# Sums over partitions by a block of ones: moving a layer norm's reductions from GpSimd to TensorE in an FNet and feed-forward kernel

## The chip, the core and the metric

The kernel runs on one core of a Trainium2 chip. The time is that of one execution on the device, in microseconds (us). The kernel before takes 683.24 us (median of three runs, 682.79 to 684.26). A core has five engines that run side by side, each through its own list of instructions in order: TensorE (PE in the profile, with its weight loads as PEld), VectorE (DVE), ScalarE (ACT), GpSimd (POOL) and SyncE (SP), which here only issues DMA transfers. An engine that has to wait for another holds up everything behind it in its own list.

## The reference

The input x has 2048 positions of 512 numbers, float32. Two sublayers follow one another, each with a layer norm ahead and a residual sum behind:

```python
a = einsum("bsd,ed->bse", x, dft_hid_re)          # x is the layer-normed input here
b = einsum("bsd,ed->bse", x, dft_hid_im)
y = einsum("ts,bse->bte", dft_seq_re, a) - einsum("ts,bse->bte", dft_seq_im, b)
...
h  = x + A(_layernorm(x), ...)                     # Fourier mixing, above
h2 = h + B(_layernorm(h), w1, w2)                  # silu(h @ w1) @ w2, F = 1792
```

The layer norm of a position needs the mean and the variance over its 512 numbers. All products are wanted in float32 accuracy.

## The kernel before, in words

**Accuracy.** Every operand of a product is split in two: ScalarE rounds it to TensorE's float32r format (the part `...h`), and VectorE subtracts to get the remainder (`...l`). `three` (lines 200 to 204) then issues three products of 128x128 by 128x512: high by high (L202), high by remainder (L203), remainder by high (L204). `rounded` (lines 149 to 160) makes the two parts; L152 is ScalarE's half and L156 or L158 VectorE's. So ahead of nearly every product stand one ScalarE and one VectorE instruction of 128x1024, and in the profile their tiles are called `ph` and `pl`.

**Stages.** The sequence mixing comes first, as `plain(0, 0)`, `fast(1, 0)`, `fast(0, 1)`, `fast(1, 1)` (the first number is the cosine or sine matrix, the second the half q of the output positions). The blocks are multiplied with seven products in place of eight where possible, which costs VectorE sums and differences (L593, L618 to L630). `mix(0)` and `mix7(1)` apply the hidden matrices to the halves, add the input, and so make h. `norm_h` (line 839) makes the second layer norm of a half. `up` and `down` are the feed-forward products. The order of the calls is: plain, fast(1,0), mix(0), fast(0,1), fast(1,1), mix7(1), up(0), down(0), up(1), down(1). The norm of half 0, called by mix(0), therefore runs on the other engines while TensorE is in fast(0,1) and fast(1,1), and that of half 1 while it is in up(0).

**The second layer norm.** After the mixing h lies transposed: 128 of the 512 numbers on the partitions, four such groups beside one another, and 512 positions along the free axis. The block of 512 positions is called tau, 0 or 1 within a half. A sum over the 512 numbers of a position is hence two additions of VectorE (L834, L835) and a sum over the partitions, which GpSimd does (L836, in `total`). This is done twice for each tau, once for the mean and once for the variance; `center` (L851) and `square` (L857) lie between. Then one row of variances goes through DRAM to be laid out over the partitions (L863, L868), VectorE makes the reciprocal roots (`root`, `finish`), they go through DRAM again (L877, L880) and `scale` multiplies (L885).

**The order.** Nothing is scheduled while it runs. Each piece of work is a function with a planned time: `step` (line 208) puts a group of products at the running clock of TensorE, 0.2265 us each, with pieces ahead of it by a lead and behind it by a delay; `at(t, f)` puts a piece at a time. `program` returns all pieces sorted by planned time, and every engine but SyncE gets its instructions in exactly that order. The planned times only fix this order: an engine starts a piece as soon as its inputs are there. The pieces of `norm_h` are at `start + d`, with `start = clock[0] + NORM_US[q][tau]` and the d of the list at L893. Pieces ahead of a product use `halves(lead, make)`: the rounding 2.2 us (GAP_US) before the lead, the remainder at the lead, most often PREP_US = 8 us.

**Pages.** All big tiles in SBUF are pages of 4 KB per partition, 51 of them (PAGES). `Plan` runs the whole program once without issuing anything, notes in which order pages are taken and when they are planned to be free, and gives each new tile the page that is planned to have been free longest. A load by SyncE waits until the last user of its page is done, and SyncE's later loads wait behind it. The loads for a group of products in `fast` (`load`, L597 to L600, issued by L328) come in threes, and `prep` (L602) makes differences of them in place (L593).

**PSUM.** `banks` (L146) gives one of four tiles of two banks each.

Of the kernel before, what the change touches and what calls it, by code (L numbers as in the profile page):

```python
# [15 lines left out]
P = 128  # L16
# [8 lines left out]
NP = NF // 2  # L25
SKEW = 2
JJ = (2, 3, 0, 1)
KEPT = (0, 1)
EPS = 1e-5
PAGES = 51  # L30
WARM = 12
MM_US = 0.2265
PREP_US = 8.0
LEADS = (((0, 14, 9, 5), (1, 15, 9, 3), 12, 11.5),
         ((0, 25, 14, 7), (1, 18.5, 7.5, 4), 17.5, 16))
LOAD_US = 18.0
FETCH_US = 13.0
NORM_US = (14, 84), (1, 14)
GAP_US = 2.2
FIRST = 0, 1, 2, 4.1, 5.15, 4.7, 5.05, 8.8, 8.2, 20, 8.9, 9.9, 21.9, 25.1, 30.5, 15  # L40
ADD_US = 15.1, 7
SUMS_US = (21.4, 5.9, 6.8, 3.7), (26.4, 5.8, 4.4, 1.2)
KEEP_US = 2, 1
FREE_US = {None: 2.0, "matmul": 4.0, "dma_start": 10.0}
ORDERED = (mybir.EngineType.PE, mybir.EngineType.DVE, mybir.EngineType.Activation, mybir.EngineType.Pool)

# [87 lines left out]
def program(nc, page, keep, small, psum, dram, x, xT, seq, hid, ffn, out):  # L134
# [244 lines left out]
    def plain(c, q):  # L379
# [71 lines left out]
        def add(name, a, b):  # L451
            nc.vector.tensor_tensor(made[name], a, b, op=ALU.add)
# [57 lines left out]
        order = [(2, 2), (1, 2), (3, 2), (1, 3), (2, 3), (3, 3), (6, 2), (7, 2), (6, 3), (7, 3), (4, 2), (4, 3), (5, 2), (5, 3)]  # L510
        for n, jj in order:
            key = "A", c, q, n, jj
            before = halves({6: 8, 4: 4.5, 7: 3.5, 5: 6.5}.get(n, PREP_US), lambda key=key, n=n: round_raw(key, -1.0 if n == 6 else 1.0))
            if n == 2:
                before += tiles_x(jj)
            if n <= 3:
                before.append((LOAD_US + {1: 0, 2: 0, 3: 4}[n], lambda n=n, jj=jj: load_b(n, jj)))
            if n == 1:
                before += [(PREP_US - 1.8, lambda jj=jj: negate(1, jj)), (PREP_US - 1.8 - 0.2, lambda jj=jj: plus(5, jj)),
                           (-1.5, lambda jj=jj: t2(jj))]  # L520
            if n == 3:
                before += [(PREP_US + 3, lambda jj=jj: negate(3, jj)), (PREP_US + 3 - 0.2, lambda jj=jj: plus(7, jj))]
            if n == 6:
                before.append((8 - 2.5, lambda jj=jj: plus(4, jj)))
            after = {
                (1, 3): [(0, lambda: copy_out("p1", acc[1]))],
                (4, 3): [(4, lambda: add("u2", acc.pop((c, q, 1, 0)), made["u2"]))],
                (2, 3): [(0, lambda: copy_out("11", acc.pop((c, q, 0, 0)))), (25, lambda: add("11", made["11"], made.pop("p1")))],
                (6, 3): [(0, lambda: copy_out("u2", acc[1]))],
                (7, 3): [(7, lambda: minus("22", acc[7])), (9, lambda: minus("u2", acc.pop(7)))],  # L530
                (5, 3): [(0, lambda: copy_out("w", acc.pop(1))), (5, lambda: add("22", made["22"], made["w"])),
                         (5.5, lambda: add("w", acc.pop((c, q, 0, 1)), made["w"]))],
            }.get((n, jj), [])
            step(12, lambda n=n, jj=jj: prod(n, jj), before, after)
        at(clock[0] + 6, ready)
        for n, v in enumerate(((0, 0), (1, 0), (1, 1), (0, 1))):
            at(clock[0] + 6 + 1.2 * n, lambda v=v: store_c(q, *v))
        for jj, (t, t3) in enumerate(((86, 96), (92, 112), (37, 54), (49, 63))):
            at(t, lambda jj=jj: early(("s", jj), lambda: sums_x(jj)))
            for n, (d, which) in enumerate(((t + 2.5, (4,)), (t3, (1, 2, 3)))):  # L540
                at(d, lambda jj=jj, n=n, which=which: early(("s", jj, n), lambda: round_s(jj, late["s", jj], which)))
                at(d + 1.5, lambda jj=jj, n=n: rest(late.pop(("s", jj, n))))
# [192 lines left out]
    def mix7(q):  # L735
# [55 lines left out]
            nc.vector.tensor_tensor(h[q, tau, e], bank[name], h[q, tau, e], op=ALU.add)  # L791

        outs = {1: [(0, 0, "Y")], 2: [(0, 0, "X")], 6: [(0, 1, "Y")], 7: [(1, 1, "V")], 5: [(1, 1, "Y")], 4: [(0, 1, "V")], 3: [(1, 0, "Y")]}
        lead = {1: 8.5, 2: 3.5, 6: 6, 7: 9, 5: 14, 4: 4, 3: 4.5}
        t = clock[0] - 43
        for n, (c, e) in enumerate(((0, 0), (0, 1), (1, 1), (1, 0))):
            at(t - 14 + n, lambda c=c, e=e: load_half(c, e))
        for n, v in enumerate((5, 7, 6, 3)):
            at(t + 1.5 * n, lambda v=v: sum_hid(v))
        for n in (1, 2, 6, 7, 5, 4, 3):  # L800
            before = halves(13.5, lambda n=n: round_hid(n))
            for i in range(2):
                before += halves(lead[n] - 1.3 * i, lambda n=n, i=i: part_of(n, i))
                if n == 1:
                    before += [(lead[1] - 0.5 - 1.3 * i, lambda i=i: negate(C[0, q, i, 0], C[0, q, i, 0])),
                               (lead[1] - 0.5 - 0.3 - 1.3 * i, lambda i=i: t1(i))]
                if n == 6:
                    before += [(lead[6] + 2.5 - 1.3 * i, lambda i=i: t2(i)), (lead[6] - 1.3 * i - 10.8, lambda i=i: t4(i))]
# [22 lines left out]
    def total(a, b, name):  # L831
# [4 lines left out]
        nc.gpsimd.partition_all_reduce(t[:, 1, :], t[:, 0, :], channels=P, reduce_op=REDUCE_ADD)  # L836
        return t

    def norm_h(q, tau, start):

        ln, sq = {}, {}
# [16 lines left out]

        def var():
            ln["v"] = total(sq.pop(0), sq.pop(1), f"v{q}{tau}")  # L860

        def row():
            nc.gpsimd.dma_start(token[0], ln["v"][0:1, 1, :])  # L863
# [26 lines left out]
                nc.gpsimd.dma_start(nd[q][tau, e], hn.pop((q, e, tau)))  # L890

        late = 6 * q
        for d, f in ((0, mean), (8, lambda: center(0)), (10, lambda: center(1)),  # L893
                     (11, lambda: square(0)), (13, lambda: square(1)), (16, var), (22, row), (25.5, gather),
                     (31 + late, root), (33.5 + late, finish), (36.5 + late, spread),
                     (45 + 2 * late, lambda: scale(0)), (47 + 2 * late, lambda: scale(1))):
            at(start + d, f)
        if q not in KEPT:
            at(start + 49 + 2 * late, store)

# [326 lines left out]
            sums_later(clock[0] + 8)  # L1227

    plain(0, 0)
    for p, t in enumerate((72, 36, -15, 69, 80, 180, -49)):  # L1230
        sums_w1(clock[0] + t, p)
    fast(1, 0)
    mix(0)
    fast(0, 1)
    fast(1, 1)
    mix7(1)
    for p, t in enumerate((-333, -296, -252, -208, 8, 60, 26)):
        make_w2(clock[0] + t, p)
    second = down(0, True), down(1, False)
    up(0, 20, lambda: next(second[0]))  # L1240
# [3 lines left out]

    nc.vector.memset(warm, 0.0)
    nc.vector.memset(lower, -0.5 * EPS)
    nc.vector.memset(upper, EPS)
    spare = keep.tile([P, 2], F32, name="spare")
    nc.gpsimd.memset(spare, 1.0)
    at(101, lambda: nc.scalar.activation(spare[:, :1], spare[:, 1:], AF.Silu))  # L1250
    at(110, lambda: nc.gpsimd.partition_all_reduce(spare[:, :1], spare[:, 1:], channels=P, reduce_op=REDUCE_ADD))
    idle = banks("idle")
    for _ in range(WARM):
# [37 lines left out]
```

## Time and profile before

| | |
|---|---|
| median of three runs | 683.24 us (682.79 to 684.26) |
| the profiled execution's own time | 681.55 us |
| its span in the profile | 679.8 us |
| granted TensorE clock | 1.000 |
| TensorE, VectorE, ScalarE, GpSimd busy | 98%, 85%, 53%, 13% |
| GpSimd sums over partitions | 8 of 3.2 to 4.1 us; those of half 0 at 224, 243, 295 and 316 us, those of half 1 between 413 and 447 us |

How to read the lines: an entry such as `DVE L156 TENSOR_TENSOR pl<-raw,ph 128x1024 fp32r<-128x1024 f32 x3` names the engine, the line of the kernel, the operation, the tile written and the tiles read (buffer numbers left out), shapes, and how many instructions are merged; the two numbers ahead are the start and the duration in us from the start of the span. A bracket such as `[4.47 <-DMA raw<-in_seq]` says that the engine had been idle 4.47 us and what ended the wait. In a list of waits, `PE m L203 <- DVE pl L156: 4.0, 3, 2.4` means that TensorE's products of line 203 into tile m waited for VectorE's line 156 for 4.0 us in all, three times, 2.4 us at the longest.

### The profile page before, as it was taken

The page shows a single profiled execution, that of the slowest core. Times are in us where ns is not written, and L with a number is a line of the kernel's source. Part 1 is how long each engine was busy: PE and PEld are TensorE (multiplying, and loading weights), DVE is VectorE, ACT ScalarE, POOL GpSimd, SP SyncE. Part 2 cuts the span into 40 slices and gives each one's busy share as a digit, 9 for nine tenths or more (in the row PEclk, how much of TensorE's full clock was granted, in tenths as well). Part 3 has the DMA queues.
Part 4 walks back from the last instruction along what each step waited for, and adds up shares of the span by engine and source line. Part 5 has one row for each costly group of instructions (what it writes and reads, how often), then busy time and mean ns, then how long its engine had stood idle before and what let it go on. Part 6 is the DMA issues. An engine that isn't in the chain of part 4 may idle for free.

```text
span 679.8 us, 8279 instructions
## 1 busy us (share of the span) xinstructions
PE 666.9 (98%) x2916; PEld 546.2 (80%) x2916; DVE 576.0 (85%) x723; ACT 362.9 (53%) x457; POOL 91.7 (13%) x108
## 2 busy tenths in 40 slices
PE   9999999999999999998999989999999999999997
PEld 6888888888888888886687867788888888888886
DVE  7899999989756998979999999877999546559964
ACT  6688747453634543442446746656655544566510
POOL 0012111211110231023112103541000000000000
PEclk9999999999999999999999999999999999999999
DMA  8948998998999367768667976497993676467802
GB/s 317 391 100 212 315 383 310 260 285 308 333 332 383 155 186 187 267 249 283 175 127 133 258 240 209 179 316 260 373 373 124 194 287 239 177 234 270 309 32 94
DMA packets 57018, 167.57 MB, mean 247 GB/s; under 512 B 6288, under 2 KB 16016, under 8 KB 56976
## 3 DMA queue, kind: packets, MB, share of 16 engines
q1 hardware_dynamic: 44752, 124.80, 51.6%
q0 software_dynamic: 11936, 41.97, 21.9%
q8 instruction: 23, 0.38, 0.2%
q10 hardware_dynamic: 288, 0.26, 0.1%
q14 instruction: 19, 0.16, 0.1%
HBM read 131.34 MB, written 32.52 MB: 241 GB/s over the span
## 4 chain that ended last, share of the span: by engine, by line
PE 81%; DVE 8%; issue 7%; DMA 2%; ACT 1%; POOL 1%; DVEq 0%; POOLq 0%; ACTq 0%
PE m L204 8%; PE m L203 8%; PE m L202 8%; PE f L204 6%; PE f L203 6%; PE f L202 6%; PE y L202 5%; PE y L204 5%; PE y L203 5%; PE c L204 3%; PE c L202 3%; PE c L203 3%; PE vx L204 2%; PE vx L203 2%; PE vx L202 2%
## 5 line engine op out<-in xcount | busy, mean ns | idle before, releaser
L152 ACT ACTIVATE ph<-raw 128x1024 fp32r<-128x1024 f32 x102 | 104.7, 1054 | 91.8 <-DVE raw L593 35.1
L156 DVE TENSOR_TENSOR pl<-raw,ph 128x1024 fp32r<-128x1024 f32 x100 | 124.4, 1260 | 10.6 <-ACT ph L152 10.1
L203 PE MATMUL m<-pl,S 128*128 128x512 f32 x192 | 75.1, 391 | 4.0 <-DVE pl L156 4.0
L204 PE MATMUL m<-ph,S 128*128 128x512 f32 x192 | 74.7, 389 | 0.0
L202 PE MATMUL m<-ph,S 128*128 128x512 f32 x192 | 74.7, 389 | 0.0
L996 DVE TENSOR_TENSOR g<-vx,g 128x512 f32<-128x512 f32 x42 | 28.9, 688 | 43.6 <-ACT g L993 18.5
L202 PE MATMUL f<-gth,wf 128*128 128x512 f32 x161 | 62.6, 389 | 0.0
L203 PE MATMUL f<-gtl,wf 128*128 128x512 f32 x161 | 62.6, 389 | 0.0
L204 PE MATMUL f<-gth,wf 128*128 128x512 f32 x161 | 62.6, 389 | 0.0
L152 ACT ACTIVATE gth<-g 128x1024 fp32r<-128x1024 f32 x42 | 43.0, 1052 | 31.1 <-DVE g L1114 12.7
L203 PE MATMUL m<-pl,X 128*128 128x512 f32 x144 | 56.1, 389 | 0.0
L202 PE MATMUL m<-ph,X 128*128 128x512 f32 x144 | 56.0, 389 | 0.0
L204 PE MATMUL m<-ph,X 128*128 128x512 f32 x144 | 56.0, 389 | 0.0
L593 DVE TENSOR_TENSOR raw<-raw,raw 128x1024 f32<-128x1024 f32 x36 | 48.0, 1334 | 7.0 <-DMA raw<-in_seq 6.4
L156 DVE TENSOR_TENSOR gtl<-g,gth 128x1024 fp32r<-128x1024 f32 x42 | 51.0, 1220 | 0.1
L203 PEld LDWEIGHTS m<-pl,S 128*128 128x128 f32 x192 | 36.0, 188 | 12.8 <-DVE pl L156 5.3
L202 PEld LDWEIGHTS m<-ph,S 128*128 128x128 f32 x192 | 36.0, 188 | 7.6
L204 PEld LDWEIGHTS m<-ph,S 128*128 128x128 f32 x192 | 36.0, 188 | 7.3
L990 ACT ACTIVATE g<-g 128x512 f32<-128x512 f32 x42 | 26.3, 627 | 22.8 <-DVE g L996 22.7
L993 ACT ACTIVATE g<-y 128x512 f32<-128x512 f32 x42 | 24.7, 593 | 20.3 <-PE y L204 20.3
L203 PEld LDWEIGHTS f<-gtl,wf 128*128 128x128 f32 x161 | 30.2, 188 | 6.3
L202 PEld LDWEIGHTS f<-gth,wf 128*128 128x128 f32 x161 | 30.2, 188 | 6.3
(350 smaller groups left out, 1566.8 us busy)
## 6 DMA issues: line engine op xcount, KB each, us to landing
raw<-in_seq SPq DMA_DIRECT2D x84, 512.0 KB, 5.7
wf<-wd SPq DMA_DIRECT2D x56, 512.0 KB, 5.4
sf<-sd SPq DMA_DIRECT2D x28, 512.0 KB, 4.6
raw<-in_seq POOLq DMA_DIRECT2D x16, 512.0 KB, 5.5
w<-in_ffn SPq DMA_DIRECT2D x28, 256.0 KB, 4.6
h<-in_xT SPq DMA_DIRECT2D x8, 512.0 KB, 6.2
hd<-h POOLq DMA_DIRECT2D x8, 512.0 KB, 6.5
r<-hd SPq DMA_DIRECT2D x8, 512.0 KB, 4.8
```

The source lines that it names most:

```text
L152: nc.scalar.activation(hi, src, AF.Copy, scale=sign)
L156: nc.vector.tensor_tensor(lo, src, hi, op=ALU.subtract)
L202: nc.tensor.matmul(acc, wh, mh, start=first, stop=False, skip_group_check=on)
L203: nc.tensor.matmul(acc, wh, ml, start=False, stop=False, skip_group_check=on)
L204: nc.tensor.matmul(acc, wl, mh, start=False, stop=last, skip_group_check=on)
L593: nc.vector.tensor_tensor(o, a, b, op=ALU.subtract)
L990: nc.scalar.activation(g[q, f][:, tau, :], src, AF.Silu)
L993: nc.scalar.activation(g[q, f][:, tau, :], src, AF.Copy)
L996: nc.vector.tensor_tensor(g[q, f][:, tau, :], src, g[q, f][:, tau, :], op=ALU.add)
```

## The change

For half 0 only (`ONES = (0,)`), `total` is no longer used. The sum over partitions is made by TensorE: VectorE makes the partial sums as before (`partial`), ScalarE rounds the 128x512 of them and VectorE takes the remainder (`split`, a new page), TensorE multiplies a block of 128x128 ones with both parts into a PSUM tile (`over_partitions`), and ScalarE copies the result to where GpSimd had put it (for the variance only one partition). The block of ones is made once, by ScalarE. Half 1 keeps GpSimd's sums.

In `norm_h` the pieces of half 0 stand at: partial sums 0 (mean) and 15 (variance; it was 16), split 2 and 17, product 5.5 and 19.5, copy 0.1 us behind the product. The chain of tau 0 starts 2 us behind the end of `mix(0)` in place of 14; that of tau 1 stays at 84.

Besides, many planned times elsewhere are other numbers: the first microseconds (FIRST, LEADS), the leads of products 4 to 7 in `plain`, the leads in `mix7`, the sums of weights, and the feed-forward's sums (SUMS_US).

```diff
+ONES = (0,)
-LEADS = (((0, 14, 9, 5), (1, 15, 9, 3), 12, 11.5),
-         ((0, 25, 14, 7), (1, 18.5, 7.5, 4), 17.5, 16))
+LEADS = (((0, 14, 10, 5.5), (1, 16.5, 9, 3.5), 12, 10.5),
+         ((0, 26.5, 13, 7), (1, 18, 8.5, 3.5), 16.5, 16))
-NORM_US = (14, 84), (1, 14)
+NORM_US = (2, 84), (1, 14)
-FIRST = 0, 1, 2, 4.1, 5.15, 4.7, 5.05, 8.8, 8.2, 20, 8.9, 9.9, 21.9, 25.1, 30.5, 15
-ADD_US = 15.1, 7
-SUMS_US = (21.4, 5.9, 6.8, 3.7), (26.4, 5.8, 4.4, 1.2)
-KEEP_US = 2, 1
+FIRST = 0, 3.2, 5.3, 4.1, 6.2, 4.7, 7.3, 7.7, 6, 17.8, 10, 14.3, 23, 25.1, 31.6, 16.1
+ADD_US = 16.1, 7
+SUMS_US = (21.4, 5.4, 7.5, 3.7), (26.4, 6.1, 3.9, 1.5)
+KEEP_US = 1, 1
...
-            before = halves({6: 8, 4: 4.5, 7: 3.5, 5: 6.5}.get(n, PREP_US), ...)
+            before = halves({6: 8.5, 4: 1.5, 7: 4, 5: 6}.get(n, PREP_US), ...)
-                           (-1.5, lambda jj=jj: t2(jj))]
+                           (-2.5, lambda jj=jj: t2(jj))]
...
-        lead = {1: 8.5, 2: 3.5, 6: 6, 7: 9, 5: 14, 4: 4, 3: 4.5}
+        lead = {1: 8.5, 2: 3.5, 6: 6, 7: 7, 5: 15, 4: 6, 3: 5.5}
-            before = halves(13.5, lambda n=n: round_hid(n))
+            before = halves(13, lambda n=n: round_hid(n))
-                    ... (lead[6] - 1.3 * i - 10.8, lambda i=i: t4(i))]
+                    ... (lead[6] - 1.3 * i - 5.8, lambda i=i: t4(i))]
...
+    ones = keep.tile([P, P], F32R, name="ones")
+    def partial(a, b, name):
+        t = page(name)
+        nc.vector.tensor_tensor(t, a, b, op=ALU.add)
+        nc.vector.tensor_tensor(t[:, 0, :], t[:, 0, :], t[:, 1, :], op=ALU.add)
+        return t
+    def split(t, name):
+        v = page(name, F32R)
+        nc.scalar.activation(v[:, 0, :], t[:, 0, :], AF.Copy)
+        nc.vector.tensor_tensor(v[:, 1, :], t[:, 0, :], v[:, 0, :], op=ALU.subtract)
+        return v
+    def over_partitions(v, name):
+        o = banks(name)[:, 0, :]
+        for n in range(2):
+            nc.tensor.matmul(o, ones, v[:, n, :], start=n == 0, stop=n == 1)
+        return o
...
+        def mean3():
+            nc.scalar.activation(ln["m"][:, 1, :], ln.pop("o"), AF.Copy)
+        def var3():
+            nc.scalar.activation(ln["v"][0:1, 1, :], ln.pop("o")[0:1, :], AF.Copy)
...
+        if q in ONES:
+            for d, f in ((2 - 2, mean1), (2, lambda: split1("m")), (5.5, mean2), (5.5 + .1, mean3),
+                         (17 - 2, var1), (17, lambda: split1("v")), (19.5, var2), (19.5 + .1, var3)):
+                at(start + d, f)
...
-    for p, t in enumerate((72, 36, -15, 69, 80, 180, -49)):
+    for p, t in enumerate((72, 36, -11, 73, 82, 178, -49)):
         sums_w1(clock[0] + t, p)
...
-    for p, t in enumerate((-333, -296, -252, -208, 8, 60, 26)):
+    for p, t in enumerate((-333, -300, -252, -208, 8, 60, 26)):
         make_w2(clock[0] + t, p)
...
+    at(100, lambda: nc.scalar.activation(ones, warm[:, :P], AF.Copy, scale=0.0, bias=1.0))
-    at(101, lambda: nc.scalar.activation(spare[:, :1], spare[:, 1:], AF.Silu))
+    at(107, lambda: nc.scalar.activation(spare[:, :1], spare[:, 1:], AF.Silu))
```

More of the change, by code (lines that the diff above doesn't have):

```diff
@@ L512, in plain @@
             key = "A", c, q, n, jj
-            before = halves({6: 8, 4: 4.5, 7: 3.5, 5: 6.5}.get(n, PREP_US), lambda key=key, n=n: round_raw(key, -1.0 if n == 6 else 1.0))
+            before = halves({6: 8.5, 4: 1.5, 7: 4, 5: 6}.get(n, PREP_US), lambda key=key, n=n: round_raw(key, -1.0 if n == 6 else 1.0))
             if n == 2:
@@ L523, in plain @@
             if n == 6:
-                before.append((8 - 2.5, lambda jj=jj: plus(4, jj)))
+                before.append((8.5 - 2.5, lambda jj=jj: plus(4, jj)))
             after = {
                 (1, 3): [(0, lambda: copy_out("p1", acc[1]))],
-                (4, 3): [(4, lambda: add("u2", acc.pop((c, q, 1, 0)), made["u2"]))],
+                (4, 3): [(7, lambda: add("u2", acc.pop((c, q, 1, 0)), made["u2"]))],
                 (2, 3): [(0, lambda: copy_out("11", acc.pop((c, q, 0, 0)))), (25, lambda: add("11", made["11"], made.pop("p1")))],
                 (6, 3): [(0, lambda: copy_out("u2", acc[1]))],
-                (7, 3): [(7, lambda: minus("22", acc[7])), (9, lambda: minus("u2", acc.pop(7)))],
+                (7, 3): [(8, lambda: minus("22", acc[7])), (8, lambda: minus("u2", acc.pop(7)))],
                 (5, 3): [(0, lambda: copy_out("w", acc.pop(1))), (5, lambda: add("22", made["22"], made["w"])),
@@ L534, in plain @@
             step(12, lambda n=n, jj=jj: prod(n, jj), before, after)
-        at(clock[0] + 6, ready)
+        at(clock[0] + 8, ready)
         for n, v in enumerate(((0, 0), (1, 0), (1, 1), (0, 1))):
-            at(clock[0] + 6 + 1.2 * n, lambda v=v: store_c(q, *v))
-        for jj, (t, t3) in enumerate(((86, 96), (92, 112), (37, 54), (49, 63))):
+            at(clock[0] + 8 + 1.2 * n, lambda v=v: store_c(q, *v))
+        for jj, (t, t3) in enumerate(((83, 90), (92, 111), (39, 54), (49, 63))):
             at(t, lambda jj=jj: early(("s", jj), lambda: sums_x(jj)))
@@ L807, in mix7 @@
                 if n == 6:
-                    before += [(lead[6] + 2.5 - 1.3 * i, lambda i=i: t2(i)), (lead[6] - 1.3 * i - 10.8, lambda i=i: t4(i))]
+                    before += [(lead[6] + 2.5 - 1.3 * i, lambda i=i: t2(i)), (lead[6] - 1.3 * i - 5.8, lambda i=i: t4(i))]
                 if n == 7:
@@ L860, in var, with mean1, split1, mean2 @@
             ln["v"] = total(sq.pop(0), sq.pop(1), f"v{q}{tau}")
+        def mean1():
+            ln["m"] = partial(h[q, tau, 0], h[q, tau, 1], f"m{q}{tau}")
+        def split1(k):
+            ln["s"] = split(ln[k], f"{k}s{q}{tau}")
+        def mean2():
+            ln["o"] = over_partitions(ln.pop("s"), f"mo{q}{tau}")
+        def mean3():
+            nc.scalar.activation(ln["m"][:, 1, :], ln.pop("o"), AF.Copy)
+        def var1():
+            ln["v"] = partial(sq.pop(0), sq.pop(1), f"v{q}{tau}")
+        def var2():
+            ln["o"] = over_partitions(ln.pop("s"), f"vo{q}{tau}")
+        def var3():
+            nc.scalar.activation(ln["v"][0:1, 1, :], ln.pop("o")[0:1, :], AF.Copy)
         def row():
@@ L892, in norm_h @@
         late = 6 * q
+        if q in ONES:
+            for d, f in ((2 - 2, mean1), (2, lambda: split1("m")), (5.5, mean2), (5.5 + .1, mean3), (17 - 2, var1), (17, lambda: split1("v")), (19.5, var2), (19.5 + .1, var3)):
+                at(start + d, f)
         for d, f in ((0, mean), (8, lambda: center(0)), (10, lambda: center(1)),
@@ L896, in norm_h @@
                      (45 + 2 * late, lambda: scale(0)), (47 + 2 * late, lambda: scale(1))):
-            at(start + d, f)
+            if not (q in ONES and f in (mean, var)):
+                at(start + d, f)
         if q not in KEPT:
```

## The prediction

> **What bounds the kernel now.** I read the page first, then the waits of TensorE, then busy time by stretch, then VectorE, SyncE and GpSimd in order of time around the stretch that loses most.
>
> ```profile
> span 679.8 us, 8279 instructions
> PE 666.9 (98%) x2916; PEld 546.2 (80%) x2916; DVE 576.0 (85%) x723; ACT 362.9 (53%) x457; POOL 91.7 (13%) x108
> ...
> PE m L203 <- DVE pl L156: 4.0, 3, 2.4
> PE y1Y L203 <- DVE pl L156: 1.3, 1, 1.3
> PE y L202 <- ACT g L993: 0.9, 2, 0.6
> PE y1V L203 <- DVE pl L156: 0.6, 1, 0.6
> ```
>
> TensorE is busy 98% of the span, so only some ten microseconds can be won at all. Nearly all its waits are for a remainder (`pl`) that VectorE made too late. The next fence shows where they lie: for each stretch the columns are TensorE, weight loads, VectorE, ScalarE and GpSimd busy, the granted clock, the DMA share and GB/s.
>
> ```profile
> 20.00:100.00 80.00, 80.00 (x354) 66.26 (x354) 75.56 (x115) 59.48 (x78) 11.88 (x18) 1.00 0.85 277
> ...
> 250.00:270.00 20.00, 20.00 (x90) 16.57 (x89) 16.78 (x25) 7.32 (x8) 3.09 (x5) 1.00 0.77 186
> 270.00:302.00 32.00, 32.00 (x143) 26.51 (x142) 31.77 (x33) 15.91 (x17) 5.15 (x3) 1.00 0.68 246
> 295.00:298.70 3.70, 3.70 (x18) 3.07 (x17) 3.70 (x3) 2.81 (x4) 3.63 (x1) 1.00 0.00 1
> 302.00:307.00 5.00, 5.00 (x23) 4.13 (x22) 0.53 (x2) 1.27 (x2) 0.00 (x0) 1.00 0.95 359
> 307.00:345.00 38.00, 33.96 (x147) 26.88 (x146) 37.50 (x44) 14.01 (x16) 8.83 (x8) 1.00 0.70 201
> 345.00:400.00 55.00, 53.98 (x236) 43.69 (x234) 54.76 (x51) 35.15 (x36) 6.61 (x8) 1.00 0.79 196
> 400.00:438.00 38.00, 35.32 (x152) 28.22 (x152) 35.26 (x41) 20.38 (x30) 15.17 (x11) 1.00 0.59 199
> ...
> 470.00:675.00 205.00, 205.00 (x906) 169.74 (x905) 154.12 (x184) 100.63 (x133) 2.13 (x4) 1.00 0.63 231
> ```
>
> TensorE is full up to 302 and again from 438 on. Between 307 and 438 it stands idle for 4.04 + 1.02 + 2.68 = 7.74 us, and there VectorE is the full engine (37.50 of 38, 54.76 of 55, 35.26 of 38). So from 307 to about 413 the end is set by VectorE's queue: a microsecond taken out of that queue, or an earlier start of it, is a microsecond off the time, as long as those 7.74 us last. Just before it, from 302 to 307, VectorE does 0.53 us of work. The cause is one chain, shown in order of time:
>
> ```profile
> 288.87 3.67 DVE L156 TENSOR_TENSOR pl<-raw,ph 128x1024 fp32r<-128x1024 f32 x3
> 294.32 5.54 DVE L156 TENSOR_TENSOR pl<-raw,ph 128x1024 fp32r<-128x1024 f32 x3
> 300.98 1.21 DVE L156 TENSOR_TENSOR pl<-raw,ph 128x1024 fp32r<-128x1024 f32 x1
> 306.66 1.23 DVE L593 TENSOR_TENSOR raw<-raw,raw 128x1024 f32<-128x1024 f32 x1 [4.47 <-DMA raw<-in_seq]
> ...
> 236.63 2.48 DVE L593 TENSOR_TENSOR raw<-raw,raw 128x1024 f32<-128x1024 f32 x2
> 316.54 4.52 DVE L593 TENSOR_TENSOR raw<-raw,raw 128x1024 f32<-128x1024 f32 x2
> ...
> 294.58 4.05 POOL L836 PARTITION_ALL_REDUCE m<-m  x1 [12.86 <-DVE m L835]
> 315.74 3.98 POOL L836 PARTITION_ALL_REDUCE v<-v  x1 [17.10 <-ACT ph L152]
> ...
> 298.74 1.75 SPq L328 DMA_DIRECT2D raw<-in_seq  x4
> ...
> SPq L328 <- DVE pl L156: 13.4, 3, 5.9
> SPq L328 <- PE m L204: 12.5, 6, 5.1
> ```
>
> While GpSimd sums over partitions at 294.58, the three `pl` that VectorE runs take 5.54 us where three took 3.67 just before. SyncE waits 5.9 us for the last of them, since it frees a page, and issues four loads at 298.74; in the 3.7 us before that the DMA engines move 1 GB/s, that is nothing. The loads land at 306.66, and VectorE has idled 4.47 us for them. At 315.74 the second sum does it again: two subtractions take 4.52 us instead of 2.48.
>
> **The change part by part.** *GpSimd's four sums of the first half go.* Those of tau 1 are the two above. What goes with the variance's sum is 4.52 − 2.48 = 2.04 us of VectorE, inside the bound stretch; with the mean's, 5.54 − 3.67 = 1.87 us ahead of the loads.
>
> One rule of the Trainium skill is weighed against this row. Its page "SBUF — State Buffer", section "Who interferes with whom", says that a GpSimd instruction which reads SBUF and a VectorE instruction with two SBUF inputs exclude each other for the whole instruction. By that rule neither subtraction could run before 315.74 + 3.98 = 319.72, and both would end at 319.72 + 2.48 = 322.20, a loss of 3.18 us; the row has them over at 316.54 + 4.52 = 321.06. By the rule the sum below would be some 1.1 us larger for each of the two terms, −5.7; the measured loss of 2.04 us decides here.
>
> *What comes in their place*, for each of four sums, with the prices of like instructions:
>
> ```profile
> L314 ACT ACTIVATE S<-s 128x512 fp32r<-128x512 f32 x16 | 9.1, 618 | 5.2 <-DVE pl L156 2.8 <-DVE s L305 2.4
> L563 ACT ACTIVATE p<-m 128x512 f32<-128x512 f32 x12 | 6.5, 594 | 14.6 <-PE m L204 12.2 <-DVE Ul L156 2.3
> L295 DVE TENSOR_TENSOR S<-s,S 128x512 fp32r<-128x512 f32 x16 | 10.2, 685 | 0.0
> ```
>
> ScalarE rounds (0.62) and copies the sums back from PSUM (0.59; for the variance one partition, the same columns), VectorE makes the remainder (0.69), TensorE runs two products of 512 columns. ScalarE's 4 × 1.21 us lie in its idle time (14.01 busy of 38). VectorE's 0.69 counts fully. TensorE's products cost 205.00 / 906 = 0.226 each, 8 × 0.226 = 1.81 us; the 7.74 us in which it stands idle hide them, and if those were gone they would cost the 1.81 in full.
>
> New waits: the products stand in TensorE's order. At tau 0 VectorE has slack. At the variance of tau 1 it is late: L834 is planned 16 us behind the mean's, and the trace has 313.55 against 292.45, 21.1 (rows below). The remainder is then ready some 2 us after TensorE gets there, and all later products wait behind it. But TensorE loses 2.36 us at 322.26 and 1.50 at 335.01 anyway, for the same late queue:
>
> ```profile
> 292.45 1.22 DVE L834 TENSOR_TENSOR m<-h,h 128x1024 f32<-128x1024 f32 x1
> 313.55 1.22 DVE L834 TENSOR_TENSOR v<-sq,sq 128x1024 f32<-128x1024 f32 x1
> ...
> 322.26 0.50 PE L203 MATMUL m<-pl,S 128*128 128x512 f32 x1 [2.36 <-DVE pl L156]
> 335.01 0.50 PE L203 MATMUL m<-pl,S 128*128 128x512 f32 x1 [1.50 <-DVE pl L156]
> ```
>
> So the wait only comes earlier: taken as 0, bounds 0 and 2. ScalarE's copy of the result waits for TensorE to finish the twelve products it is in (12 × 0.226 = 2.7 us at most), and the rounding of `ph` queues behind that; with ScalarE busy 14 of 38 I take 0, bound 2.7.
>
> *The chain of tau 0 moves from 14 to 2 us behind the mixing.* Four scalings of VectorE move from 270–275, where it is full, into 250–270, where it was busy 16.78 of 20; the two stretched runs beside the sums of tau 0 go as well:
>
> ```profile
> 225.24 4.52 DVE L593 TENSOR_TENSOR raw<-raw,raw 128x1024 f32<-128x1024 f32 x2
> 243.16 5.54 DVE L156 TENSOR_TENSOR pl<-raw,ph 128x1024 fp32r<-128x1024 f32 x3
> ...
> 270.00 1.29 DVE L885 TENSOR_TENSOR hr<-hr,v 128x512 f32<-128x512 f32 x2
> 273.81 1.28 DVE L885 TENSOR_TENSOR hr<-hr,v 128x512 f32<-128x512 f32 x2
> ```
>
> That takes up to 1.29 + 1.28 = 2.57 us out of the full queue that ends in the four loads at 298.74. How far these move: at least by 1.87 − 0.69 = 1.18; at most to 295.0, 3.7 us, since before that the DMA engines were busy with earlier loads (share 0.00 only from 295.0). SyncE waits for TensorE about as long as for VectorE there (12.5 against 13.4), which a faster VectorE doesn't shorten; I take 2.1, nearer the lower end.
>
> *All the other moved pieces* (start, lead times of the first half, sums of weights, the second half's mixing, the feed-forward) change only the order on ScalarE, VectorE and the queues: an engine starts a piece when its inputs are there, not at its planned time. In 20–100 and 470–675 TensorE is full with VectorE at 75.56 of 80 and 154.12 of 205: cost 0, covered by remainders made ahead; without that cover one late remainder costs about its own 1.2 us. The rounding ahead of product 4 (lead 4.5 to 1.5) is the tightest. In the second half's mixing the order is shuffled inside a stretch that VectorE fills; the waits of 1.3 and 0.6 us there may vanish, but the same work then ends at the same time: 0, bound −1.9.
>
> **The sum.** −(2.04 − 0.69) = −1.35 for the variance, −2.1 for the loads: −3.45 us. The profiled execution's own time of 681.55 (span 679.8 and 1.75 around it) becomes 678.1. The runs' median, 683.24, is 1.7 above that execution; taken off it, 679.8.
>
> **Rivals.**
> 1. *The loads stay.* Another page than the one VectorE frees, or TensorE's releases, holds SyncE until 298.7. Then only the 1.35 us of the variance are left, and a hold of ScalarE behind TensorE may eat part: 681.9 to 683.2, say 682.6. For it: 12.5 us of SyncE's waits are for TensorE. Against: the last of them, at 298.74, follows the stretched `pl`.
> 2. *Slower: the loads come later.* Each sum takes one more page for its two parts, from the same 51, and every page drawn after gets another predecessor. If SyncE's first load in that block gets a page that the next `pl` frees (300.98 + 1.21 = 302.2), it is issued 3.5 us later, and VectorE's queue starts at 310.2: +3.5 − 1.35 = +2.15, 685.4. It decides from where the first subtraction of the last pass starts later than 306.66 + 1.35 = 308.0. Against: the mean's and the variance's pages are short-lived.
> 3. *TensorE pays and nothing comes back.* If VectorE's relief is eaten by the new waits, the full engine has 1.81 us more: 685.0. The Trainium skill's page "GPSIMD Engine Reference", section "4.1 Engine selection", speaks for it, since it gives sums along partitions to GpSimd. Against: 7.74 us of idle TensorE in just that stretch.
> 4. *More.* Both bounds are reached (−1.35 − 3.7 = −5.05), or the reordered mixing gives back its 1.9 beside the sum (−5.35): 678.0.
>
> **How the numbers follow.** Forecast 52%, rival 1 18%, 2 10%, 3 5%, 4 15%. The likeliest one's own range is 678.2 (−5.05) to 681.9 (−1.35). The range 677.2 to 683.6 holds the forecast, most of rival 4 and rival 1, and leaves out rivals 2 and 3 and a little of 4. About 0.2% (1.4 us) is what a measurement of this kernel can tell from no change: the forecast and rival 4 are faster but for a little of the forecast's upper end, rival 1 is mostly "same": faster 0.68, same 0.18, slower 0.14.
>
> **What would show it.** Right: no GpSimd sum and no stretched VectorE instruction between 207 and 345; four loads issued between 295 and 297.6 and the first subtraction of that pass at 303–305.5; TensorE's waits between 307 and 345 down from 4.0 to about 2 us, some of it ahead of a product with the block of ones; the waits around 421–437, where GpSimd still sums, about as before. Wrong: loads still at 298.7 or later, new waits of TensorE before 300 or after 440, or ScalarE idle before the copies from PSUM with VectorE idle behind it.

## The result, and the profile after

The kernel after takes 678.69 us (median of 4 executions, 678.01 to 679.05), the kernel before on the same chip 683.01: a ratio of 0.9932, with a 95% interval of 0.9915 to 0.9949. Two later series of the same kernel gave 679.22 (ratio 0.9952, 0.9936 to 0.9967) and 679.64 (0.9953, 0.9937 to 0.9969). The median of all 22 executions is 679.22. The profiled execution took 678.37, against 681.55 before: −3.18.

From the page of the kernel after, its span and busy times:

```profile
span 676.6 us, 8293 instructions
PE 667.7 (99%) x2924; PEld 547.2 (81%) x2924; DVE 571.2 (84%) x727; ACT 367.5 (54%) x466; POOL 75.6 (11%) x104
```

VectorE has 4.8 us less work although it has four remainders more, GpSimd 16.1 us less, TensorE eight products more. The waits of TensorE in the kernel after (us in all, times, longest; line numbers are shifted by the change, so that L156 is now L157, L593 is L594 and L202 to L204 are L203 to L205):

```profile
PE y1Y L203 <- DVE h L792: 1.6, 1, 1.6
PE y L203 <- ACT g L1041: 1.2, 2, 0.9
PE vx L203 <- DVE g L1044: 0.4, 1, 0.4
PE y1Y L204 <- DVE pl L157: 0.3, 1, 0.3
PE vo L859 <- DVE vs L852: 0.2, 1, 0.2
```

The 4.0 us that products into `m` waited for a remainder are gone altogether. What is left belongs to the second half's mixing (`y1Y`) and to the feed-forward's first products (`y`, `vx`). The one new wait, 0.2 us, stands ahead of a product with the block of ones. Busy time by stretch of the kernel after (TensorE, weight loads, VectorE, ScalarE, GpSimd, granted clock, DMA share, GB/s):

```profile
302.00:307.00 5.00, 5.00 (x23) 4.13 (x22) 3.88 (x5) 2.01 (x2) 0.00 (x0) 1.00 0.83 289
307.00:345.00 38.00, 38.00 (x169) 31.44 (x168) 36.90 (x46) 16.17 (x19) 4.92 (x7) 1.00 0.72 205
```

From 307 to 345 TensorE now does 169 products in the 38 us, where it did 147: 22 × 0.226 = 4.97 us of work more. That is the gain in work done by 345, and it is larger than the 4.04 us of idle time that the page showed there, since a product behind a wait also takes longer. From 302 to 307 VectorE works 3.88 us in place of 0.53. The same chain as before, in order of time:

```profile
294.62 0.68 DVE L852 TENSOR_TENSOR ms<-m,ms 128x512 fp32r<-128x512 f32 x1
295.22 1.22 DVE L157 TENSOR_TENSOR pl<-raw,ph 128x1024 fp32r<-128x1024 f32 x1
298.35 1.23 DVE L157 TENSOR_TENSOR pl<-raw,ph 128x1024 fp32r<-128x1024 f32 x1 [1.92 <-ACT ph L153]
303.66 1.22 DVE L594 TENSOR_TENSOR raw<-raw,raw 128x1024 f32<-128x1024 f32 x1 [1.12 <-DMA raw<-in_seq]
313.54 0.68 DVE L852 TENSOR_TENSOR vs<-v,vs 128x512 fp32r<-128x512 f32 x1
314.14 2.47 DVE L594 TENSOR_TENSOR raw<-raw,raw 128x1024 f32<-128x1024 f32 x2
...
296.50 1.28 SPq L329 DMA_DIRECT2D raw<-in_seq  x3
...
298.81 0.63 PE L859 MATMUL mo<-ms,ones 128*128 128x512 f32 x2
315.62 0.63 PE L859 MATMUL vo<-vs,ones 128*128 128x512 f32 x2
```

No VectorE instruction is stretched there. SyncE issues the first three of the four loads from 296.50 on (298.74 before) and the fourth at 298.78. The first subtraction of the last pass starts at 303.66 (306.66 before): it waits for the third of these loads, issued at 297.36, where before it waited for the fourth, issued at 300.07 (they land 6.2 and 6.5 us behind their issue). The pair of subtractions takes 2.47 us in place of 4.52. It ends at 314.14 + 2.47 = 316.61, against 321.06: VectorE is 4.45 us ahead. The products with the block of ones wait for nothing at tau 1.

The whole account by TensorE: I added up, over the trace, the time between the starts of neighbouring products beyond 0.2267 us. Call this the time that TensorE loses. It was 13.45 us before (2.78 in the first 20 us, 5.09 between 302 and 345, 5.53 between 345 and 438) and is 8.45 after (2.41, 0.03 and 5.48; 0.52 is new between 207 and 250, most of it at the product with ones that waits). That is −5.00; the eight products add 8 × 0.2267 = 1.81; together −3.19, and the profiled executions differ by −3.18. So the gain comes out of one stretch, 302 to 345.

### The profile page after: what moved, and what is told of

Same layout as the page of the kernel before. It is cut to its first block, busy times and chain, and to the rows that moved or that the text cites. A ratio compares the mean times of both kernels' runs of the same rounds, so it can differ in the third digit from the quotient of the medians.

```text
span 676.6 us, 8293 instructions
## 1 busy us (share of the span) xinstructions
PE 667.7 (99%) x2924; PEld 547.2 (81%) x2924; DVE 571.2 (84%) x727; ACT 367.5 (54%) x466; POOL 75.6 (11%) x104
## 4 chain that ended last, share of the span: by engine, by line
PE 83%; DVE 10%; DMA 4%; issue 2%; ACT 1%; POOL 0%; DVEq 0%; ACTq 0%
PE m L203 9%; PE m L205 9%; PE m L204 9%; PE f L204 6%; PE f L203 6%; PE f L205 6%; PE y L203 5%; PE y L205 5%; PE y L204 5%; DMA raw<-in_seq 4%; PE c L203 3%; PE c L205 3%; PE c L204 3%; DVE pl L157 3%; PE vx L204 2%; PE vx L203 2%
## 5 line engine op out<-in xcount | busy, mean ns | idle before, releaser
L157 DVE TENSOR_TENSOR pl<-raw,ph 128x1024 fp32r<-128x1024 f32 x100 | 120.5, 1219 | 10.8 <-ACT ph L153 10.5
L205 PE MATMUL m<-ph,S 128*128 128x512 f32 x192 | 74.7, 389 | 0.0
L203 PE MATMUL m<-ph,S 128*128 128x512 f32 x192 | 74.7, 389 | 0.0
L204 PE MATMUL m<-pl,S 128*128 128x512 f32 x192 | 74.7, 389 | 0.0
L203 PE MATMUL f<-gth,wf 128*128 128x512 f32 x161 | 62.6, 389 | 0.0
L204 PE MATMUL f<-gtl,wf 128*128 128x512 f32 x161 | 62.6, 389 | 0.0
L205 PE MATMUL f<-gth,wf 128*128 128x512 f32 x161 | 62.6, 389 | 0.0
L205 PE MATMUL m<-ph,X 128*128 128x512 f32 x144 | 56.0, 389 | 0.0
L203 PE MATMUL m<-ph,X 128*128 128x512 f32 x144 | 56.0, 389 | 0.0
L204 PE MATMUL m<-pl,X 128*128 128x512 f32 x144 | 56.0, 389 | 0.0
L157 DVE TENSOR_TENSOR gtl<-g,gth 128x1024 fp32r<-128x1024 f32 x42 | 50.8, 1217 | 0.0
L594 DVE TENSOR_TENSOR raw<-raw,raw 128x1024 f32<-128x1024 f32 x36 | 43.9, 1220 | 3.6 <-DMA raw<-in_seq 3.0
L205 PEld LDWEIGHTS m<-ph,S 128*128 128x128 f32 x192 | 36.0, 188 | 7.6
L203 PEld LDWEIGHTS m<-ph,S 128*128 128x128 f32 x192 | 36.0, 188 | 7.5
L204 PEld LDWEIGHTS m<-pl,S 128*128 128x128 f32 x192 | 36.0, 188 | 7.5
L203 PEld LDWEIGHTS f<-gth,wf 128*128 128x128 f32 x161 | 30.2, 188 | 6.3
L205 PEld LDWEIGHTS f<-gth,wf 128*128 128x128 f32 x161 | 30.2, 188 | 6.3
```

The source lines that it names most:

```text
L157: nc.vector.tensor_tensor(lo, src, hi, op=ALU.subtract)
L203: nc.tensor.matmul(acc, wh, mh, start=first, stop=False, skip_group_check=on)
L204: nc.tensor.matmul(acc, wh, ml, start=False, stop=False, skip_group_check=on)
L205: nc.tensor.matmul(acc, wl, mh, start=False, stop=last, skip_group_check=on)
L594: nc.vector.tensor_tensor(o, a, b, op=ALU.subtract)
```

## The experiments

All ratios are to the kernel before on the same chip. Three theories stood against one another at first: that the gain comes from GpSimd's sums no longer stretching VectorE's instructions; that it comes from GpSimd's own queue being free earlier; and that it comes from the moved pieces, with the ones as a bystander.

**The ones and the early chain, nothing else** (the kernel before, with the eight pieces of half 0's sums and the chain of tau 0 at 2 us; all other planned times as before).

```diff
+ONES = (0,)
-NORM_US = (14, 84), (1, 14)
+NORM_US = (2, 84), (1, 14)
```

> The kernel before (683.0 us) with the sums of half 0 on TensorE and the chain of tau 0 at 2 us; every other planned time as before. Theory (GpSimd's sums at tau 1 stretch VectorE's two-input instructions and through them hold SyncE's loads): most of the gain comes, 679.5 to 680.5 us, TensorE's waits between 307 and 345 us below 1 us, no VectorE instruction of 3.26 us before 400. Rival A (the gain is in the moved pieces): 682 to 683.

Measured: 678.85 us, ratio 0.9945 (0.9931 to 0.9959), a little faster than expected. No VectorE instruction is stretched before 400 us, and TensorE loses 0.03 us between 302 and 345. The interval overlaps all three of the full change's, so the rest of the moved pieces is worth nothing that these runs can tell.

**The moved pieces without the ones** (the kernel after, GpSimd's sums put back).

```diff
-ONES = (0,)
+ONES = ()
```

> The changed kernel (678.7 us) with GpSimd's sums kept in half 0: only the moved pieces are left of the change. Theory: 681.5 to 682.5, the stretched instructions of 3.26 us are back beside all four sums, and of the gain only the start's 0.7 us and a lighter VectorE queue ahead of tau 1 remain. Rival A (the moved pieces carry it): 678.5 to 679.5.

Measured: 687.45 us, ratio 1.0072 (1.0047 to 1.0097): slower than before, which nothing in the expectation foresaw. So the gain is not in the moved pieces, the early chain among them; without the ones they do harm, and the next run shows that the early chain by itself does.

**The early chain alone** (the kernel before, only `NORM_US`).

```diff
-NORM_US = (14, 84), (1, 14)
+NORM_US = (2, 84), (1, 14)
```

> The kernel before with nothing but the chain of tau 0 at 2 us behind the mixing in place of 14; all sums stay on GpSimd. Theory (the two sums at tau 1 are what costs): VectorE's queue ahead of the four loads gets lighter, but the stretched instructions stay: 681.5 to 683, at most 1 us faster. Rival D (the earlier chain is the gain, the ones are along for the ride): 679 to 680.

Measured: 685.29 us, ratio 1.0040 (1.0026 to 1.0054): slower by 2.8 us, which neither side of the expectation had. In order of time, its VectorE, ScalarE and TensorE:

```profile
260.71 1.23 DVE L156 TENSOR_TENSOR pl<-raw,ph 128x1024 fp32r<-128x1024 f32 x1 [4.15 <-ACT ph L152]
...
259.61 2.01 ACT L152 ACTIVATE ph<-raw 128x1024 fp32r<-128x1024 f32 x2 [5.52 <-PE m L204]
...
268.57 0.50 PE L203 MATMUL m<-pl,S 128*128 128x512 f32 x1 [3.33 <-DVE pl L156]
270.17 0.63 PE L202 MATMUL m<-ph,S 128*128 128x512 f32 x1
270.60 0.63 PE L203 MATMUL m<-pl,S 128*128 128x512 f32 x1
```

VectorE stands idle for a rounding of ScalarE, which itself had waited 5.52 us for products of TensorE, and eight microseconds later TensorE waits 3.33 us, at a place where the kernel before has no wait. Why that rounding stands behind those products was not settled. The wait costs more than its own length here: behind it, from 269.8 to 273 us, the granted clock is 0.52, and products start 0.43 us apart in place of 0.227, some 1.7 us in all. With the ones in, the same early chain gives 0.9945: between these two kernels, which differ in the ones alone, lie 0.0095, some 6.5 us. In their traces TensorE loses 5.25 against 1.39 us between 250 and 302, and 9.02 against 5.07 behind 302; so about half of the difference arises behind the sums of tau 0, ahead of those of tau 1.

**GpSimd's sums of tau 1 beside the products with ones** (the kernel after; the result of the sum is overwritten).

```diff
+    def beside(t, tau):
+        if tau == 1:
+            nc.gpsimd.partition_all_reduce(t[:, 1, :], t[:, 0, :], channels=P, reduce_op=REDUCE_ADD)
...
+            beside(ln["m"], tau)      # in mean1
+            beside(ln["v"], tau)      # in var1
```

> The changed kernel with GpSimd's sum made as well at tau 1, mean and variance; its result is overwritten by the copy from PSUM, nothing reads it. Theory: two stretched VectorE instructions of 3.26 us are back (+2.0 us each), 681 to 682.5 us. Rival B (what helped is a sum that is ready earlier, or one engine less in the chain): 678.7, since the chain is still TensorE's.

Measured: 683.58 us (12 executions, 679.72 to 684.64), ratio 1.0007 (0.9993 to 1.0021). The whole gain is gone, and a little more than was expected, though every sum that counts is still made by TensorE. The profiled execution is its fastest one. VectorE and TensorE in it, in order of time:

```profile
294.31 2.73 DVE L852 TENSOR_TENSOR ms<-m,ms 128x512 fp32r<-128x512 f32 x1
314.26 2.73 DVE L852 TENSOR_TENSOR vs<-v,vs 128x512 fp32r<-128x512 f32 x1
...
317.05 0.50 PE L859 MATMUL vo<-vs,ones 128*128 128x512 f32 x1 [1.33 <-DVE vs L852]
```

The stretch now falls on the two remainders, 0.68 to 2.73 us each, and the second of them makes TensorE wait ahead of the product with ones. This trace accounts for only a part of what the series lost: TensorE loses 1.67 us in it between 302 and 345, against 0.03 in the kernel after.

**GpSimd held as long by writes alone** (the same two places, nine memsets of 128x512 each in place of the sum).

```diff
+        if tau == 1:
+            for _ in range(9):
+                nc.gpsimd.memset(t[:, 1, :], 0.0)
```

> The changed kernel with GpSimd kept busy at the same two places by nine memsets of 128x512 each in place of a sum: it writes SBUF and reads nothing; its queue is held for about as long. Theory (it is GpSimd's reading beside VectorE's two inputs that stretches): no stretched VectorE instruction, 678.5 to 679.3 us. Rival C (GpSimd's queue being held, with the accumulating loads behind it, is what costs): 681 to 682.5 as with the sum beside.

Measured: 681.09 us (12 executions), ratio 0.9978 (0.9964 to 0.9992). GpSimd and VectorE in order of time:

```profile
293.17 5.21 POOL L865 MEMSET m<- 128x512 f32 x9 [17.92 <-DVE m L845]
312.85 5.20 POOL L865 MEMSET v<- 128x512 f32 x9 [14.48 <-DVE v L845]
318.07 0.89 POOL L609 DMA_DIRECT2D raw<-in_seq  x1
...
294.48 0.69 DVE L852 TENSOR_TENSOR ms<-m,ms 128x512 fp32r<-128x512 f32 x1 [0.30 <-ACT ms L851]
313.70 0.68 DVE L852 TENSOR_TENSOR vs<-v,vs 128x512 fp32r<-128x512 f32 x1
```

GpSimd is busy longer than with the sums, and no VectorE instruction beside it is stretched. Yet the time is not the 678.5 to 679.3 us that the theory gave; it lies in the range named for rival C. Against the sums (1.0007) it is 0.0029 better, so the stretching makes some 2.0 us of the sums' harm, with an uncertainty of about 1.4. Against the kernel after it is 0.0025 to 0.0046 worse, and its interval is clear of the first series but overlaps the two later ones a little: the blocked queue (its load L609 is issued at 318.07, in the kernel after at 314.18) may cost about as much again, which these runs leave open. The trace, of the fastest of the twelve executions (679.09 us), doesn't show where: TensorE loses only 0.27 us in it between 302 and 345.

**One of the two sums at a time**, with the kernel after beside them on the same chip. First the mean's:

```diff
+            beside(ln["m"], tau)      # in mean1; nothing in var1
```

> The kernel after, with GpSimd's sum of tau 1's mean made beside the products; its result is overwritten by the copy from PSUM, so it only takes up GpSimd and the memory ports. This puts back one of the two stretches that the prediction priced: the one ahead of the four loads. By the prediction's terms the loads come 1.2 to 3.7 us later and the kernel loses 2.1 us against the kernel after, near 680.7 (ratio to before about 0.9975), with a VectorE instruction of about 2.7 us at the mean's remainder and none at the variance's. If most of what both sums together cost (about 4.4 us in the timed runs) comes from the loads behind the mean, this run is at 682 or more and the one with the variance's sum alone near 679.5. If both matter about equally, both runs are near 681.

Then the variance's:

```diff
+            beside(ln["v"], tau)      # in var1; nothing in mean1
```

> The kernel after, with GpSimd's sum of tau 1's variance alone made beside the products, its result overwritten. By the prediction's term for the variance this costs what one stretched instruction loses, 2.04 us, near 680.6 (ratio about 0.9970), with a VectorE instruction of about 2.7 us at the variance's remainder and a wait of TensorE of about 1.5 us ahead of the products with the block of ones that follow. If TensorE's work before that product covers the late remainder, it costs nothing: near 678.9. If all of the loss of both sums comes from here, 682 or more.

And the kernel after:

> The kernel after itself, on the same chip as the two runs beside it, so that they are compared with it: 678.0 to 679.5, ratio to before 0.993 to 0.996. If its profiled execution shows TensorE waiting near 267 us again, that wait belongs to the landing of transfers and differs from execution to execution; if it doesn't, the one seen earlier was a rare case.

Measured: mean 680.65 us, ratio 0.9972 (0.9955 to 0.9989); variance 681.18, 0.9981 (0.9960 to 1.0002); kernel after 679.64, 0.9953 (0.9937 to 0.9969). By the ratios the mean's sum costs 0.0019, or 1.3 us, and the variance's 0.0028, or 1.9 us (1.0 and 1.5 us by the medians), each with an uncertainty of about 1.7. Neither is clearly told from nothing by itself, nor the two from one another, nor their sum of 3.2 us from the 3.7 us (0.0054) that both cost in one kernel. The mean's run is where the prediction's terms had it, at 680.7, but the kernel after beside it was a little slower than reckoned (at most 679.5). In order of time, VectorE, GpSimd, SyncE and TensorE of the kernel with the mean's sum:

```profile
294.70 2.73 DVE L852 TENSOR_TENSOR ms<-m,ms 128x512 fp32r<-128x512 f32 x1
306.14 1.23 DVE L594 TENSOR_TENSOR raw<-raw,raw 128x1024 f32<-128x1024 f32 x1 [3.33 <-DMA raw<-in_seq]
...
293.83 4.06 POOL L864 PARTITION_ALL_REDUCE m<-m  x1 [17.03 <-PE m L205]
...
298.63 1.76 SPq L329 DMA_DIRECT2D raw<-in_seq  x4
...
316.77 0.50 PE L859 MATMUL vo<-vs,ones 128*128 128x512 f32 x1 [0.51 <-DVE vs L852]
```

Up to the remainder this execution runs level with the first profile of the kernel after (294.70 against 294.62). The one stretched instruction puts the loads from 296.50 to 298.63, the first subtraction from 303.66 to 306.14, and VectorE's idle time ahead of it from 1.12 to 3.33 us. That is the chain of the prediction, switched on by one instruction of GpSimd. TensorE waits 0.51 us ahead of the variance's product, and loses 7.46 us in all behind 302, against 5.48, 4.85 and 5.28 in the three profiles of the kernel after: some 2 us, about what the prediction had. The variance's sum starts when these loads have long been issued. In its trace, which runs some 4 us later from 110 us on for another wait of TensorE (2.90 us, for ScalarE), the remainder is stretched, and the wait that was expected to be about 1.5 us is 0.22:

```profile
318.08 2.73 DVE L852 TENSOR_TENSOR vs<-v,vs 128x512 fp32r<-128x512 f32 x1
...
317.29 3.98 POOL L864 PARTITION_ALL_REDUCE v<-v  x1 [37.76 <-DVE v L845]
...
320.86 0.50 PE L859 MATMUL vo<-vs,ones 128*128 128x512 f32 x1 [0.22 <-DVE vs L852]
```

**Four times the products with ones** (the kernel after; each pair issued four times over, every time as a new sum: 24 products more).

```diff
-        for n in range(2):
-            nc.tensor.matmul(o, ones, v[:, n, :], start=n == 0, stop=n == 1)
+        for _ in range(4):
+            for n in range(2):
+                nc.tensor.matmul(o, ones, v[:, n, :], start=n == 0, stop=n == 1)
```

> The changed kernel with each pair of products with the ones issued four times over (24 more products, 24 x 0.226 = 5.4 us of TensorE). Theory (TensorE waits for VectorE between 345 and 438 anyway, 3.5 us there in the changed kernel): only what exceeds that idle time shows, +1 to +2.5 us, and the waits at 397 to 400 vanish. Rival E (TensorE is the bound, its products cost their time): +5.4 us.

Beside it ran the kernel after once more:

> The changed kernel itself, as the measure for the others on this chip. 678 to 679 us; ratio to the kernel before 0.992 to 0.995.

Measured: 684.32 us, ratio 1.0028 (1.0014 to 1.0042), against 679.22 (0.2 us above its expected range). The 24 products are 24 × 0.2267 = 5.44 us of TensorE, and they cost 5.1. Next to nothing hid them: that is rival E, and the theory's +1 to +2.5 is refuted. Busy time beside them, from the stretches of that run (columns as above):

```profile
307.00:345.00 38.00, 38.00 (x169) 31.41 (x168) 36.16 (x45) 17.20 (x21) 4.92 (x7) 1.00 0.69 214
345.00:405.00 60.00, 58.51 (x257) 47.80 (x256) 58.28 (x53) 36.16 (x37) 6.61 (x8) 1.00 0.76 187
```

TensorE of the run with 24 more products, in order of time:

```profile
302.51 2.03 PE L860 MATMUL mo<-ms,ones 128*128 128x512 f32 x8
320.72 2.03 PE L860 MATMUL vo<-vs,ones 128*128 128x512 f32 x8
403.00 0.47 PE L203 MATMUL y1Y<-ph,H3h 128*128 128x512 f32 x1 [1.34 <-DVE h L792]
425.15 0.50 PE L203 MATMUL y<-T5h,sf 128*128 128x512 f32 x1 [0.87 <-ACT g L1042]
434.01 0.50 PE L203 MATMUL vx<-T7h,sf 128*128 128x512 f32 x1 [0.41 <-DVE g L1045]
```

Its main waits behind 400 us are those of the kernel after, whose rows are:

```profile
397.17 0.47 PE L203 MATMUL y1Y<-ph,H3h 128*128 128x512 f32 x1 [1.62 <-DVE h L792]
419.31 0.50 PE L203 MATMUL y<-T5h,sf 128*128 128x512 f32 x1 [0.86 <-ACT g L1041]
428.17 0.50 PE L203 MATMUL vx<-T7h,sf 128*128 128x512 f32 x1 [0.37 <-DVE g L1044]
```

They moved some 6 us to the right and kept nearly their size: behind 345 TensorE loses 4.8 us here and 5.5 in the kernel after. So at most some 0.7 of the 5.44 us that are added ahead of these waits is taken out of them, and the rest is paid.

The profiled execution of the repeated kernel took 680.99 us and has a wait that the first profile of the same kernel lacks, from TensorE in order of time:

```profile
269.56 0.50 PE L204 MATMUL m<-pl,S 128*128 128x512 f32 x1 [1.04 <-DVE pl L157]
```

Between 255 and 270 us VectorE waits 3.5 us for a transfer there, in the first profile 1.0. The third profile (680.59 us) has no wait of TensorE there, but others ahead of 150 us, where VectorE waits 4.5 us for transfers between 100 and 160 (0.5 in the first). One execution of this kernel differs from the next by up to 3.4 us, and in these profiles by such waits; a difference of one microsecond is read from the timed series, not from two profiles.

**The ones for the second half too** (the kernel after; the sums of half 1 go into the unused half of a PSUM tile that the feed-forward's products hold).

```diff
-ONES = (0,)
+ONES = (0, 1)
...
-                bank[p, "Y"] = banks(f"y{q}{p}")[:, 0, :]
+                y2 = banks(f"y{q}{p}")
+                bank[p, "Y"], half["o"] = y2[:, 0, :], y2[:, 1, :]
```

> The changed kernel with the ones for half 1 too (its PSUM tile is the unused half of a y tile of the first feed-forward). The four sums of GpSimd at 410 to 447 us go and with them VectorE's stretched instructions (3.26, 2.13, 2.66 us) there. Theory: TensorE's three waits at 419, 428 and 434 (2.05 us together) shrink to below 0.7; eight more products cost 1.8 us, hidden as far as idle time is left: 676.5 to 679. Rival E (products cost their time): 679.5 to 680.5; it may also wait in new places, since TensorE stands in the products' way during the feed-forward.

Measured: 686.56 us, ratio 1.0061 (1.0044 to 1.0079): slower, and far outside both expected ranges. No stretched instruction is left in the whole trace, but TensorE, in order of time, waits:

```profile
411.59 0.50 PE L203 MATMUL y<-T5h,sf 128*128 128x512 f32 x1 [2.01 <-ACT g L1044]
422.79 0.50 PE L203 MATMUL y<-T5h,sf 128*128 128x512 f32 x1 [0.89 <-ACT g L1044]
430.41 0.50 PE L203 MATMUL y<-T6h,sf 128*128 128x512 f32 x1 [1.37 <-ACT m L897]
445.94 0.50 PE L203 MATMUL y<-T5h,sf 128*128 128x512 f32 x1 [0.68 <-ACT v L906]
```

Two of these waits are for the copies of the sums out of PSUM (L897, L906): products into the shared tile stand behind them. Why the wait for ScalarE's `g` at 411.59 is 2.01 us long was not isolated. So the change is not good wherever GpSimd sums; in half 0 the sums get a PSUM tile of their own, in `up` they share one with products that wait. No kernel that ran was shown to be faster than the kernel after.

## Why the prediction was right, point by point

The forecast was 679.8 us, the first series gave 678.69, the later ones 679.22 and 679.64; the profile was to fall by 3.45 us and fell by 3.18. That the gain comes from taking GpSimd's sums away is shown: the other parts of the change give none without that (1.0072, 1.0040), and with both sums of tau 1 back beside the products the gain is gone (1.0007). The way through VectorE and the loads is seen in the traces. How much is the stretching and how much GpSimd's held queue is not settled, and the prediction knew only the first. That the size came out so close is in part luck: two errors cancel, as follows.

- *VectorE's queue sets the end from 307 us on.* Right as far as 345: VectorE came 4.45 us earlier, and TensorE got back all but 0.03 of the 5.09 us that it lost there. Wrong behind that: 24 products added to TensorE cost 5.1 us although VectorE was busy 58.28 of the 60 us from 345 to 405 beside them. A full VectorE was read as one that bounds by itself.
- *The variance, −1.35 us.* From the first subtraction to the end of the pair it was 321.06 − 306.66 = 14.40 us and is 316.61 − 303.66 = 12.95: −1.45. The sum put back alone, beside the remainder that stays, should cost the stretch of 2.04; it costs 1.9 by the ratios.
- *The loads, −2.1 us.* SyncE issues the first three 2.24 us earlier. The subtraction starts 3.0 us earlier, since it also waits for the third load in place of the fourth, which was not foreseen; the term is 0.9 too small. The subtraction and three loads lie in the windows that were named. The fourth load, at 298.78, does not, but the subtraction doesn't wait for it. Put back alone, the mean's sum costs 1.3 us by the ratios, with an uncertainty that takes in the 2.1; in its trace the delay of the loads is there in full (idle 3.33 against 1.12), and TensorE loses some 2 us more behind 302. The 1.87 us that were read for this stretch compare merged rows of three; the stretched instruction by itself lost 2.04, like the other.
- *TensorE's eight products, taken as 0.* This is the step that failed. The reasoning was that "the 7.74 us in which it stands idle hide them"; the waits between 307 and 345 that were to hide them are gone, and those behind 345 absorb little of what is added. By the run with 24 more, eight cost 5.1 / 3 = 1.7 us. The prediction had that price, 1.81, for the case that the idle time was gone, and this case is what happened. The gross gain was not 3.45 but 5.00 by the time that TensorE loses, which made up for it.
- *The wait for the variance's product, taken as 0, bounds 0 and 2.* Right: 0 at tau 1, 0.2 us at tau 0. The 2 us wait that was expected to come earlier did not come at all, since VectorE was 4.45 us earlier there. The wait at tau 0 is a new one ahead of 300 us, which was named as a sign of being wrong; at 0.2 us it decides nothing.
- *ScalarE's hold, taken as 0, bound 2.7.* It exists: ScalarE idles 1.15 us for the product before it copies the mean at 299.48, and VectorE 0.53 us for that copy at 300.11. The first subtraction behind it still waits 1.12 us for its loads, so the hold costs nothing there.
- *The early chain, counted as relief of the full stretch.* Alone it costs 2.8 us. The prediction priced the sums of tau 1 only; between the kernel with the early chain and the one with the ones as well lie 6.5 us, of which both sums of tau 1 are 3.7 by the run that puts them back. The remaining 2.8 us were not isolated; the time that TensorE loses between 250 and 302, the lower clock behind the long wait included, speaks for tau 0.
- *All other moved pieces, 0.* Right within what can be told: 0.9945 without them against 0.9932 to 0.9953.
- *The waits at 421 to 437 about as before.* Right: by the starts of the products there 1.89 us before, 2.06 after. *TensorE's waits between 307 and 345 down to about 2:* they went to zero.
- *The rivals.* The loads came earlier, so neither the first nor the second held. The third, TensorE pays and nothing comes back, was half true: it pays, and more than it pays comes back. The Trainium skill's page "GPSIMD Engine Reference", section "4.1 Engine selection", which spoke for it, is not borne out in half 0 of this kernel (0.9932 to 0.9953); with the ones in both halves the kernel is slower (1.0061), there with a shared PSUM tile.

## What to carry to other kernels

An engine that is "full" over a stretch need not be what bounds it: put extra work on the other engine and see whether it costs its full time, as 24 products of 0.2267 us nearly did here. A late instruction that frees a page is worth what the transfers behind it are worth, and a sum on GpSimd is worth what it holds up, the VectorE instruction beside it and perhaps GpSimd's own queue, not its own 4 us. And moving a reduction to a fuller engine has to be tried place by place: in half 0 it gave 0.5 to 0.7%, in both halves together, with a shared PSUM tile, it lost 0.6%.

## What the runs showed of the hardware that was not expected

What a sum of GpSimd over partitions costs VectorE depends on when VectorE's next instruction with two inputs in SBUF begins, not on its length. A remainder of 0.68 us becomes 2.73 in each of the four cases that were made, +2.05, and a 128x1024 instruction of 1.22 us becomes 3.26 before the change, +2.04. But where such an instruction begins later, it loses less. From the kernel after, VectorE and GpSimd in order of time, at a sum of half 1:

```profile
440.76 0.68 DVE L1044 TENSOR_TENSOR g<-vx,g 128x512 f32<-128x512 f32 x1
441.36 2.67 DVE L157 TENSOR_TENSOR Vl<-v,Vh 128x1024 fp32r<-128x1024 f32 x1
...
439.81 4.13 POOL L837 PARTITION_ALL_REDUCE v<-v  x1 [0.34 <-DVE v L836]
```

`Vl` begins 1.55 us behind the start of the sum and loses 1.45; `g`, of whose two inputs one is in PSUM, is not stretched. In all the traces a stretched instruction of 1.22 us ends 0.07 to 0.09 us behind the recorded end of the sum and one of 0.68 us 0.44 to 0.46 ahead of it: both are held until some 1.14 us before that end. The sum is held as well: where a two-input VectorE instruction is running when the sum starts, the sum ends 3.09 to 3.11 us behind the end of that instruction, and its recorded length of 3.87 to 4.13 varies with how long that one still ran.

The Trainium skill's page "SBUF — State Buffer", section "Who interferes with whom", has the two exclude each other for the whole instruction. For the sum that waits, the rows agree. For VectorE, the remainder beside the mean's sum (293.83 + 4.06 = 297.89) would by that have ended at 297.89 + 0.68 = 298.57; it ended at 294.70 + 2.73 = 297.43. So the rows show that VectorE is held for a large part of the sum, and not for all of its recorded length; spans on GpSimd are rough, however. The same section says that a GpSimd instruction which only writes SBUF does not disturb a VectorE instruction with two SBUF inputs, and the run with memsets agrees: 0.69 and 0.68 us beside 5.2 us of writing.

Timed executions of one and the same kernel lay between 677.64 and 680.99 us, and the profiles of three of them show their waits at different places. With GpSimd's sums back, the spread was 679.72 to 684.64, with the profiled execution at the very bottom; what makes the others of that series slower than the profiled one was not seen, since only one execution has a trace. The mean granted clock does not tell them apart: it is 0.997 in five of the twelve, 681.77 to 684.46 us, and 0.999 or 1.000 in the rest, up to 684.64. The profiled execution is also the fastest of its series with the memsets, with the moved pieces alone and with the ones in both halves, so these traces show less than the series lost.
